# A kernel for attention and two expert layers: the first layer's opening and the order of its router's operations

## The chip, the core and the metric

The kernel runs on one core of a Trainium2 chip. The metric is the time of one execution on the device in microseconds, as the median of several runs.

The engines are named as in the profile: PE (TensorE, matrix products), DVE (VectorE), ACT (ScalarE), POOL (GpSimd, which also issues indirect transfers) and SP (SyncE, which issues plain transfers). Each works through its own list of instructions in the order in which it is written, and waits on semaphores for the others.

## What is computed

Attention over 4 batches, 12 heads, 448 positions and head width 64, then two layers of experts one after the other, each over the same 1792 tokens of width 768 with 8 experts of inner width 1024. All inputs and outputs are float32.

```python
scores = (q @ k.T) / sqrt(64), causal mask, softmax, @ v        # 4 x 12 heads
x = the heads side by side                                      # [1792, 768]

# first layer: the router compares directions
logits = (x / |x|) @ (emb / |emb|).T / tau
e = argmax(logits);  g = softmax(logits)[e]
x = g * (relu(x @ w1[e]) @ w2[e])

# second layer: the router is a product, with a bias by modality
logits = x @ w_gate + modality_bias[modality_id]
e = argmax(logits);  g = softmax(logits)[e]
out = g * (relu(x @ w1[e]) @ w2[e])
```

## The kernel before, in words

Everything that enters a large product is split into a high part (a rounded copy, `xh`, `w1h`, `w2h`, `hh`) and the rest (`xl`, `w1l`, `w2l`, `hl`). A product is then three: high by high, high input by low weight, low input by high weight. ACT makes the high parts by casting, DVE the low parts by subtracting.

**Attention** (loop at L799) goes through 24 pairs of heads in a software pipeline. Its last turns also bring the last batch of the first router: sums of squares (`route_ss`), transposes of x (`route_t`, L513) and the products for the logits (`route_l`, L524). `warm` (L783) puts products on PE whose result nobody reads.

**The router of the first layer** (`route1_head` L590, `route1_tail` L620, `finish_route` L193, `argmax` L208): transposed logits, scaling, argmax with a one-hot `r1ohb`, a count over tokens by products with `triu` and `ones` (L631, L633), slots, the softmax's value for the chosen expert (a subtraction, an exponential on ACT, a sum and a reciprocal), and a scatter of one row per token into a list by expert in DRAM (`meta1`). These functions are generators: each `yield` ends a step, and who drives them decides what stands between two steps. For the last batch the driver is `last_route1` (L1462).

**Tables.** `Lead.order` (L256) sorts the experts, `table` (L1220) turns counts into a list of blocks and issues the gathers of the next blocks' rows (`gather_m`, `gather_x`); its second half finds the second expert, whose number POOL copies (`load_second`, L1211) so that SP can load its weights. `switches` (L1265) writes `t_tab`, a table that says at each block whether the expert changes. The other engines read it into registers to branch.

**Blocks.** The first layer takes 128 tokens of one expert at a time. `first_block` (L1151) is block 0, `section(j)` (L1299) is block j. A block is two products with `w1` (`up`, L967, 18 matmuls each), a ReLU on ACT, transposes of the result (`h_transposes`, or `h_turn` and `h_turned`) and the product with `w2` (`down`, L1029, 48 matmuls). In section j the product with `w2` belongs to block j - 1. Where the expert changes, `split_next` (L1286) splits new weights, and `load_next` (L1198) issues the loads of the ones behind them. Block 0 begins while the router still finishes: `step()` in `first_block` runs one step of `last_route1` between two pieces of the block.

**The second router.** After a block of the first layer its outputs are routed for the second one: transposes (`route_t2`), logits (`route_l2`, product with `wg`), argmax to a one-hot `ob` (`route_a`, L1084), the count (`route_p`, L1105), slots and scatter (`route_b`). These are spread over the section of a later block. `prep(m, j)` (L948) makes `xh` and `xl` of block j; from block 3 on DVE first turns the gathered rows (`x_squares`, L945).

## Time and profile before

| | us |
|---|---|
| median of 3 runs | 942.31 |
| fastest, slowest run | 939.3, 949.46 |
| profiled execution | 932.79 |
| its span in the profile | 931.1 |
| PE, DVE, ACT, POOL busy in the span | 864.4, 699.8, 428.4, 478.0 |

The profile is one execution; times in it count from its span's start. Attention takes about the first 245 us, the first expert layer goes to about 620, the second one to the end. In a timeline a line gives the start, the time that it took, engine, source line, operation, output and inputs, how many in a row, and in brackets how long the engine stood before it and what released it. `issue` is time for which the profile shows no wait. Bracketed waits on an engine cost time only where another engine then waits for that one.

### The profile page before, as it was taken

What the parts mean: (1) busy time and instruction counts of PE and PEld (TensorE: products, weight loads), DVE (VectorE), ACT (ScalarE), POOL (GpSimd) and SP (SyncE); (2) the same over time, 40 slices, a digit from 0 to 9 for tenths busy, and PEclk for the clock granted to TensorE, in tenths of its full rate; (3) what the DMA queues carried; (4) which work ended last, traced back from release to release, by engine and by line L of the source; (5) the groups of instructions that cost most, each with busy time, mean ns of one, the idle gap of its engine ahead of it and who ended that gap; (6) DMA issues with size and microseconds to landing.
All of it is one profiled execution on the core that took longest, in us unless ns stands there. A gap on an engine that the chain in (4) does not pass through costs nothing. (4 is left out here: it accounts for less than half of the span.)

```text
span 931.1 us, 21180 instructions
## 1 busy us (share of the span) xinstructions
PE 864.4 (93%) x7010; PEld 752.0 (81%) x7010; DVE 699.8 (75%) x1800; ACT 428.4 (46%) x779; POOL 478.0 (51%) x477
## 2 busy tenths in 40 slices
PE   4999998988788999999999999979989999999994
PEld 3778777776576989988999888977779999898894
DVE  7999998997875766787657783467767578985793
ACT  3767866776434745575445552244111231412313
POOL 7867497674265153544645554312634454554541
PEclk9999998999899999999999999999989999999998
DMA  6899987889737765686515751110181115511110
GB/s 190 163 165 172 210 181 158 178 182 177 235 93 262 277 239 169 221 293 223 186 39 195 276 184 46 45 36 22 56 306 55 53 55 170 175 56 48 58 38 17
DMA packets 114454, 137.45 MB, mean 148 GB/s; under 512 B 78381, under 2 KB 82787, under 8 KB 114288
## 3 DMA queue, kind: packets, MB, share of 16 engines
q1 hardware_dynamic: 101376, 108.76, 42.8%
q0 software_dynamic: 12912, 26.83, 9.1%
q8 instruction: 61, 1.00, 0.4%
q14 instruction: 105, 0.86, 0.3%
HBM read 101.48 MB, written 19.92 MB: 130 GB/s over the span
## 5 line engine op out<-in xcount | busy, mean ns | idle before, releaser
L764 POOL DMA_INDIRECT xg<-x,xi x128 | 135.2, 1056 | 97.4 <-DMA x<-yb,mg 55.5
L973 PE MATMUL h<-w1h,xh 128*128 128x512 f32 x408 | 164.5, 403 | 1.9 <-ACT xh L957 1.1
L975 PE MATMUL h<-w1h,xl 128*128 128x512 f32 x408 | 161.1, 395 | 1.0 <-DVE xl L958 1.0
L974 PE MATMUL h<-w1l,xh 128*128 128x512 f32 x408 | 161.2, 395 | 0.7 <-DVE w1l L714 0.7
L1035 PE MATMUL o<-w2h,hh 128*128 128x384 f32 x528 | 140.4, 347 | 1.8 <-issue 1.6
L1035 PE MATMUL o<-w2h,hl 128*128 128x384 f32 x528 | 137.5, 341 | 2.7 <-DVE hl L988 1.5
L1035 PE MATMUL o<-w2l,hh 128*128 128x384 f32 x528 | 136.8, 340 | 1.4 <-issue 1.3
L1015 DVE STREAM_TRANSPOSE hs<-h 32x256 f32<-32x256 f32 x240 | 107.1, 446 | 21.5 <-PE h L975 8.3
L434 ACT ACTIVATE ex<-sc,nm 112x112 f32<-112x112 f32 (+1 forms) x192 | 83.9, 502 | 67.7 <-DVE nm L429 65.7
L1035 PEld LDWEIGHTS o<-w2h,hl 128*128 128x128 f32 x528 | 96.7, 190 | 3.6 <-DVE hl L988 2.1
L1035 PEld LDWEIGHTS o<-w2h,hh 128*128 128x128 f32 x528 | 95.8, 192 | 4.8 <-issue 3.0
L1035 PEld LDWEIGHTS o<-w2l,hh 128*128 128x128 f32 x528 | 97.1, 191 | 2.3 <-issue 1.8
L1021 ACT ACTIVATE hh<-hs 128x512 fp32r<-128x512 f32 x30 | 18.4, 630 | 174.1 <-PE o L1035 112.1
L975 PEld LDWEIGHTS h<-w1h,xl 128*128 128x128 f32 x408 | 76.9, 189 | 19.4 <-DVE xl L958 2.0
L974 PEld LDWEIGHTS h<-w1l,xh 128*128 128x128 f32 x408 | 77.2, 189 | 17.9 <-DVE w1l L714 2.6
L973 PEld LDWEIGHTS h<-w1h,xh 128*128 128x128 f32 x408 | 77.1, 189 | 17.7 <-ACT xh L957 1.3
L714 DVE TENSOR_TENSOR w1l<-w1r,w1h 128x1024 fp32r<-128x1024 f32 x66 | 76.6, 1220 | 9.3 <-ACT w1h L712 8.0
L429 DVE TENSOR_REDUCE nm<-sc 112x1 f32<-112x112 f32 (+1 forms) x192 | 75.1, 437 | 9.5 <-PE sc L424 8.7
L714 DVE TENSOR_TENSOR w2l<-w2r,w2h 128x768 fp32r<-128x768 f32 x82 | 72.4, 951 | 7.8 <-ACT w2h L712 6.8
L946 DVE STREAM_TRANSPOSE xr<-xg 128x768 f32<-128x768 f32 x32 | 52.0, 1626 | 22.6 <-DMA xg<-x,xi 15.8
L712 ACT CAST w1h<-w1r 128x1024 fp32r<-128x1024 f32 x64 | 62.5, 1047 | 9.5 <-PE h L975 5.0
L712 ACT CAST w2h<-w2r 128x768 fp32r<-128x768 f32 x82 | 61.5, 845 | 0.8 <-ACTq L1374 0.6
(327 smaller groups left out, 1919.2 us busy)
## 6 DMA issues: line engine op xcount, KB each, us to landing
w1r<-in_w1a SPq DMA_DIRECT2D x48, 512.0 KB
w2r<-in_w2a SPq DMA_DIRECT2D x64, 384.0 KB
r<-in_kqP SPq DMA_DIRECT2D x24, 448.0 KB
w1r<-in_w1b SPq DMA_DIRECT2D x18, 512.0 KB
w2r<-in_w2b SPq DMA_DIRECT2D x24, 384.0 KB
vr<-in_vh SPq DMA_DIRECT2D x24, 224.0 KB
x<-xb SPq DMA_DIRECT2D x16, 336.0 KB
xg<-x,xi POOLq DMA_INDIRECT x128
```

The costliest lines, as they stand in the source:

```text
L429: vec.tensor_reduce(out=nms[h][:, c : c + 1], in_=scs[h, c][:CP, : CP * (c + 1)], axis=AX.X, op=ALU.min)
L434: act.activation(dst, scs.pop((h, c))[:CP, :n], AF.Exp, bias=nms[h][:, c : c + 1], scale=-1.0)
L712: act.copy(hi[k], r[k])
L714: vec.tensor_sub(lo[k], r[k], hi[k].bitcast(F32))
L764: pool.indirect_dma_start(out=xgs[j % 3][:, q * (D // Q) : (q + 1) * (D // Q)], out_offset=None, in_=quarters, in_offset=IND(ap=xi[:, q : ...
L946: vec.transpose(xr.rearrange("p k (q r) -> p q k r", q=Q), xgs[j % 3].rearrange("p (q r k) -> p q k r", q=Q, k=KD))
L973: pe.matmul(hps, lhsT=xh[:, c], rhs=w1h[c][:, ns], start=(c == 0), stop=False)
L974: pe.matmul(hps, lhsT=xh[:, c], rhs=w1l[c][:, ns], start=False, stop=False)
L975: pe.matmul(hps, lhsT=xl[:, c], rhs=w1h[c][:, ns], start=False, stop=(c == KD - 1))
L1015: vec.transpose(hr[cols, :, rows], hps[rows, q * 256 : (q + 1) * 256].rearrange("p (c k) -> p k c", c=QR))
L1021: act.activation(hh[k], part, AF.Relu)
L1035: pe.matmul(ops[:, n, :384], lhsT=h[f // KH][:, f % KH], rhs=w[f][:, n * 384 : (n + 1) * 384], start=(f == 0 and st == 0), stop=(f == KF - ...
```

## The change

In the attention's last turns 15 more `warm` products are put on PE: 7 more ahead of the last transposes, 3 behind them and 5 behind the last logits. In block 0 the first product is `up_late`: all 12 matmuls of `xh` stand ahead of the 6 of `xl`. The router's last batch takes its logits and its argmax, up to the one-hot, in two steps ahead of the block's matmuls, without the expert order between its operations; the softmax's subtraction and exponential move ahead of the count; the expert order follows the scatter. Of `w2` in block 0 only slice 0 gets its low part early. `table` is cut in two by a `yield`: the half that finds the second expert, and with it POOL's copy, stands behind the low parts of `w2`. In section 1 the logits of the second router stand ahead of the transposes, and in section 2 `route_a` stands as a whole ahead of block 3's `prep`.

```diff
--- before.py
+++ after.py
@@ -624,6 +624,10 @@
         vec.tensor_copy(ohb[:, :NCH], oh[:CP])
         base = small.tile([P, E], F32, tag="r1base", name="r1base" + nm)
         vec.tensor_add(base, cnt1, slot8)
+        gate = finish_route(lg, mx, CP, NCH, nm, mts[b][:, :, 2])
+        if b == B - 1:
+            for _ in range(2):
+                next(gate)
         yield
         yield ALIGN
         pr = side()[:, : (NCH + 1) * E].rearrange("p (c e) -> p c e", e=E)
@@ -646,7 +650,7 @@
         vec.tensor_copy(si, sf)
         yield
         mt = mts[b]
-        yield from finish_route(lg, mx, CP, NCH, nm, mt[:, :, 2])
+        yield from gate
         if b == 0:
             yield from lead1.choose(cnt1)
         elif b == 1:
@@ -832,7 +836,7 @@
         if 0 <= t < NPR:
             halves_lo(t, (1,))
         if g == NPR + 2:
-            warm(ps_T, "T", WV)
+            warm(ps_T, "T", WV + 7)
         if 0 <= r < NPR:
             if r == NPR - 1:
                 for c in range(NCH):
@@ -840,6 +844,8 @@
                 last_root = route_root(B - 1)
                 next(last_root)
             route_t(r, xbs[r // PB])
+            if r == NPR - 1:
+                warm(ps_T, "T", 3)
             if r == NPR - 2:
                 for c in range(NCH):
                     route_ss(B - 1, c, xbs[B - 1], 1)
@@ -870,6 +876,8 @@
             values(v, 1)
         if 0 <= r < NPR:
             route_l(r)
+            if r == NPR - 1:
+                warm(ps_T, "T", 5)
         if 0 <= v < NPR:
             combine(v, xbs[v // PB])
         if g < NPR:
@@ -964,6 +972,19 @@
                 next(meanwhile, None)
             vec.tensor_sub(xl, xr, xh.bitcast(F32))
 
+    def up_late(j, n, between):
+
+        xh, xl = xhs[j % 2], xls[j % 2]
+        hps = ps_h.tile([P, 512], F32, tag="h", name="h")
+        ns = slice(n * 512, (n + 1) * 512)
+        for c in range(KD):
+            pe.matmul(hps, lhsT=xh[:, c], rhs=w1h[c][:, ns], start=(c == 0), stop=False)
+            pe.matmul(hps, lhsT=xh[:, c], rhs=w1l[c][:, ns], start=False, stop=False)
+        for c in range(KD):
+            between.get(c, lambda: None)()
+            pe.matmul(hps, lhsT=xl[:, c], rhs=w1h[c][:, ns], start=False, stop=(c == KD - 1))
+        return hps
+
     def up(j, n, between={}):
         xh, xl = xhs[j % 2], xls[j % 2]
         hps = ps_h.tile([P, 512], F32, tag="h", name="h")
@@ -1155,14 +1176,18 @@
         if not ahead:
             prep(m, 0)
             step()
-        split_away(range(0 if m.routed else 3, away))
-        h0 = up(0, 0, {2: step, 3: step} if ahead else {3: step})
+        if m.routed:
+            split_w(2, range(away), range(1))
+            h0 = up_late(0, 0, {2: step})
+        else:
+            split_away(range(3, away))
+            h0 = up(0, 0, {2: step, 3: step} if ahead else {3: step})
         split_w(2, range(away, KF if ahead else 6), ())
         if ahead:
             split_w(2, (), range(away, away + 2))
         step()
         relu(0, h0)
-        if not ahead:
+        if not ahead and not m.routed:
             split_w(2, (), range(away, away + 1))
         h1 = up(0, 1, {4: lambda: prep(m, 1), 5: step} if ahead else {4: step})
         relu(1, h1)
@@ -1171,8 +1196,10 @@
         h_transposes()
         if ahead:
             split_w(2, (), range(away + 3, KF))
+        if m.routed:
+            split_w(2, (6, 7), range(1, KF))
         drain(steps)
-        if not ahead:
+        if not ahead and not m.routed:
             split_w(2, (6, 7), range(away + 1, KF))
         if not ahead:
             switches(m, m.tab0)
@@ -1248,6 +1275,7 @@
                     gather(1)
             gather(2)
 
+        yield
         nz = small.tile([P, E], F32, tag="t_nz", name="t_nz" + m.m, bufs=1)
         vec.tensor_single_scalar(nz, m.nb, 0.5, op=ALU.is_ge)
         vec.tensor_tensor(out=t64, in0=m.lead.gt, in1=nz[:, None, :].to_broadcast([P, E, E]), op=ALU.mult)
@@ -1317,6 +1345,8 @@
                 m.gather_m(j + 4)
                 m.gather_r(j + 4)
             ra, rb = (route_a(), chain(route_g(), route_b())) if finish else (iter(()), iter(()))
+            if j == 2:
+                drain(ra)
             if FIRSTQ <= j + 1 < MAXB:
                 prep(m, j + 1, ra, FIRSTQ + 1)
             h0 = up(j, 0)
@@ -1355,10 +1385,11 @@
                 down(m, m.mg(j - 1), h_split)
             else:
                 if m.routed:
+                    route_l2()
                     h_turn()
                 (h_turned if m.routed else h_split)()
                 pass_on()
-            if begin:
+            if begin and j > 1:
                 route_l2()
             vec.tensor_copy(gt, m.mg(j))
 
@@ -1428,17 +1459,22 @@
         route_p()
         drain(route_b())
         yield
-        table(m2, both)
+        drain(table(m2, both))
 
     def last_route1(both):
         head = route1_head(B - 1)
-        for _ in range(2):
+        for _ in range(6):
             next(head)
         yield
-        together(head, lead1.order(cnt1))
+        drain(head)
         yield from (y for y in route1_tail(B - 1) if y == ALIGN)
         yield
-        table(m1, None)
+        drain(lead1.order(cnt1))
+        rest = table(m1, None)
+        next(rest)
+        yield
+        yield
+        drain(rest)
 
     drain(last_root)
     m1.gather_early((1,), 3 * S)
```

DVE in block 0, from the low part of x on (`ld_` is the expert order, `r1` and `am_` the router, `w2l` low weights), before:

```order
L958 TENSOR_TENSOR xl_5808<-xt,xh_5807 128x384 x2
L260 SCALAR_TENSOR_TENSOR ld_key<-cnt_194,iota_127 128x8
L605 COPY r1lor_5864<-t 112x32
L262 SCALAR_TENSOR_TENSOR ld_key<-ld_onem_212,ld_key 128x8
L607 TENSOR_TENSOR r1lgr_5845<-t,r1lor_5864 112x32
L264 TENSOR_TENSOR ld_mat<-ld_key 128x64
L613 TENSOR_TENSOR r1lgr_5845<-r1lgr_5845,r1nrr_5724 112x32
...
L624 CAST r1ohb_186<-am_ohr_5872 112x32
L626 TENSOR_TENSOR r1baser_5888<-cnt_194,slot_130 128x8
...
L723 TENSOR_TENSOR w2l_5799<-w2r_5496,w2h_5801 128x768
L723 TENSOR_TENSOR w2l_5800<-w2r_5497,w2h_5802 128x768
L636 TENSOR_TENSOR r1slr_5910<-t,r1baser_5888 112x32
```

DVE at the same place now:

```order
L605 COPY r1lor_5868<-t 112x32
L607 TENSOR_TENSOR r1lgr_5862<-t,r1lor_5868 112x32
L613 TENSOR_TENSOR r1lgr_5862<-r1lgr_5862,r1nrr_5731 112x32
L966 TENSOR_TENSOR xl_5825<-xt,xh_5824 128x384 x2
L215 TENSOR_REDUCE am_mxr_5884<-r1lgr_5862 112x4
...
L624 CAST r1ohb_186<-am_ohr_5885 112x32
L626 TENSOR_TENSOR r1baser_5893<-cnt_194,slot_130 128x8
L196 TENSOR_TENSOR fr_shr_5895<-r1lgr_5862,am_mxr_5884 112x32
L718 TENSOR_TENSOR w2l_5816<-w2r_5496,w2h_5818 128x768
L640 TENSOR_TENSOR r1slr_5922<-t,r1baser_5893 112x32
...
L206 RECIPROCAL mt_160<-fr_smr_5930 112x4
L260 SCALAR_TENSOR_TENSOR ld_key<-cnt_194,iota_127 128x8
```

Three router operations come ahead of `xl`, the others behind it in one piece, the subtraction for the exponential (`fr_shr`) ahead of the first `w2l`, and the order (`ld_key`) behind the reciprocal that ends the softmax.

DVE further on in block 0, now: behind the last operation of the table's first half stand `hl`, seven `w2l` (three of them shown) and the table's second half up to `ld_mxm`, from which the second expert's number is copied. Before, the second half stood ahead of `hl`.

```order
L1267 TENSOR_SCALAR t_idqm_322<-t_basem_5975,qrow 128x22
...
L1009 TENSOR_TENSOR hl_5811<-ht,hh_5813 128x512
L1009 TENSOR_TENSOR hl_5812<-ht,hh_5814 128x512
L718 TENSOR_TENSOR w2l_5817<-w2r_5497,w2h_5819 128x768
L718 TENSOR_TENSOR w2l_5786<-w2r_5498,w2h_5820 128x768
...
L718 TENSOR_TENSOR w2l_5781<-w2r_5503,w2h_5787 128x768
...
L1280 TENSOR_SCALAR t_nzm_6042<-t_nbm_319 128x8
L1281 TENSOR_TENSOR t_64m_5965<-ld_gtm_216,t_nzm_6042 128x64
L1282 TENSOR_REDUCE t_nxem_323<-t_64m_5965 128x8
...
L1288 TENSOR_REDUCE ld_mxm_214<-t_nzm_6042 128x1
```

All that finds the second expert has moved behind the low weights.

ACT in block 0, before (`fr_shr` is the exponential, `xh` and `w2h` are casts):

```order
L957 CAST xh_5807<-xt 128x384 x2
L722 CAST w2h_5801<-w2r_5496 128x768
L722 CAST w2h_5802<-w2r_5497 128x768
L198 ACTIVATE fr_shr_5918<-fr_shr_5918 112x32
L712 CAST w2h_5803<-w2r_5498 128x768
```

and ACT in block 0 now:

```order
L965 CAST xh_5824<-xt 128x384 x2
L198 ACTIVATE fr_shr_5895<-fr_shr_5895 112x32
L716 CAST w2h_5818<-w2r_5496 128x768
L716 CAST w2h_5819<-w2r_5497 128x768
L716 CAST w2h_5820<-w2r_5498 128x768
```

The exponential has moved ahead of the first two casts of `w2h`.

DVE in section 2 (`xr` and `xl` are block 3's x, the others but `gt` belong to `route_a`), before:

```order
L1363 COPY gt<-mg_340 128x8
L946 STREAM_TRANSPOSE xr<-xg_338 128x4x6x32
L1088 TENSOR_SCALAR r2md<-yq 128x1
L1090 TENSOR_SCALAR r2bs<-mb,r2md 128x8
L1092 SCALAR_TENSOR_TENSOR r2bs<-mb,yq,r2bs 128x8
L965 TENSOR_TENSOR xl_5763<-xr,xh_5762 128x768
L1096 TENSOR_TENSOR lg_5786<-pl,r2bs 128x8
L215 TENSOR_REDUCE mx_5788<-lg_5786 128x1
```

and DVE in section 2 now:

```order
L1394 COPY gt<-mg_340 128x8
L1109 TENSOR_SCALAR r2md<-yq 128x1
L1111 TENSOR_SCALAR r2bs<-mb,r2md 128x8
L1113 SCALAR_TENSOR_TENSOR r2bs<-mb,yq,r2bs 128x8
L1117 TENSOR_TENSOR lg_5803<-pl,r2bs 128x8
...
L1122 CAST ob_5801<-oh_5799 128x8
L1123 COPY yo_5797<-yq 128x8
L954 STREAM_TRANSPOSE xr<-xg_338 128x4x6x32
L973 TENSOR_TENSOR xl_5780<-xr,xh_5779 128x768
```

`route_a` with its one-hot `ob` now ends ahead of `xr`.

## Rows read from the trace of the kernel before

**Rows 1.** Windows view: stretch, busy us of PE (x instructions), PEclk, DMA share, GB/s

```profile
250.00:255.00 5.00, 3.97 (x11) 0.50 0.35 129
```

**Rows 2.** Timeline of PE, end of attention and block 0

```profile
242.23 1.47 PE L787 MATMUL warm<-mask,ones 112*128 112x512 bf16 x6
245.11 0.60 PE L517 MATMUL tb<-ident,xb 112*128 112x112 f32 x4 [1.41 <-DVE xb L508]
...
248.61 0.36 PE L601 MATMUL t<-ident,lgs 16*112 16x16 f32 x4 [1.24 <-issue]
...
252.69 0.80 PE L975 MATMUL h<-w1h,xl 128*128 128x512 f32 x1 [1.01 <-DVE xl L958]
...
255.88 0.19 PE L631 MATMUL t<-r1ohb,triu 112*128 112x40 bf16 x1
...
262.17 0.40 PE L975 MATMUL h<-w1h,xl 128*128 128x512 f32 x1
...
266.50 0.61 PE L1035 MATMUL o<-w2h,hl 128*128 128x384 f32 x2 [0.90 <-DVE hl L988]
```

**Rows 3.** Timeline of DVE, block 0

```profile
252.08 1.02 DVE L958 TENSOR_TENSOR xl<-xt,xh 128x384 fp32r<-128x384 f32 x2 [0.57 <-ACT w2h L722]
253.02 0.16 DVE L260 SCALAR_TENSOR_TENSOR ld_key<-cnt,iota 128x8 f32<-128x8 f32 x1
...
255.50 0.23 DVE L282 TENSOR_TENSOR ld_gtm<-ld_gtm,ld_key 128x64 f32<-128x64 f32 x1
...
258.77 0.18 DVE L202 TENSOR_REDUCE fr_smr<-fr_shr 112x4 f32<-112x32 f32 x1 [0.30 <-ACT fr_shr L198]
258.99 0.17 DVE L204 TENSOR_SCALAR fr_smr<-fr_smr 112x4 f32<-112x4 f32 x1
...
264.68 0.16 DVE L1260 TENSOR_REDUCE ld_mxm<-t_nzm 128x1 f32<-128x8 f32 x1
...
265.77 1.28 DVE L988 TENSOR_TENSOR hl<-ht,hh 128x512 fp32r<-128x512 f32 x2
266.96 4.42 DVE L714 TENSOR_TENSOR w2l<-w2r,w2h 128x768 fp32r<-128x768 f32 x5
...
274.37 0.14 DVE L1284 CAST t_tabm<-t_chgm 1x1 int32<-1x1 f32 x1
```

**Rows 4.** Timeline of ACT, casts of block 0 and x of block 1

```profile
250.88 1.57 ACT L722 CAST w2h<-w2r 128x768 fp32r<-128x768 f32 x2
...
275.82 0.86 ACT L957 CAST xh<-xt 128x384 fp32r<-128x384 f32 x2 [0.27 <-issue]
```

**Rows 5.** Timeline of PE, blocks 1 to 4

```profile
276.35 0.50 PE L973 MATMUL h<-w1h,xh 128*128 128x512 f32 x1 [1.11 <-ACT xh L957]
...
302.04 0.17 PE L1108 MATMUL pr<-ob,triu 128*128 128x8 bf16 x1 [1.42 <-DVE ob L1101]
...
308.03 0.52 PE L1035 MATMUL o<-w2h,hl 128*128 128x384 f32 x2
308.38 1.06 PE L997 MATMUL ht<-ident,hs 128*128 128x128 f32 x8
...
317.64 1.12 PE L1071 MATMUL yt<-ident,yb 128*128 128x128 f32 x6
```

**Rows 6.** Timeline of POOL, the second expert's number

```profile
272.23 0.18 POOL L164 TENSOR_SCALAR t_secondm<-ld_mxm 1x1 int32<-1x1 f32 x1
```

**Rows 7.** Timeline of SP, loads of weights

```profile
274.54 6.24 SPq L701 DMA_DIRECT2D w1r<-in_w1a  x6
291.53 5.73 SPq L701 DMA_DIRECT2D w2r<-in_w2a  x8
```

**Rows 8.** Timelines of ACT and DVE, the third expert's weights

```profile
311.95 2.15 ACT L712 CAST w1h<-w1r 128x1024 fp32r<-128x1024 f32 x2 [1.04 <-SPq L1294]
...
316.86 1.23 DVE L1005 TENSOR_TENSOR hl<-ht,hh 128x512 fp32r<-128x512 f32 x2
```

## The prediction

> **What bounds the kernel now.** I read four views: busy time by stretch, then the timelines of TensorE (PE), VectorE (DVE) and the queues from the end of attention to the fourth block of the first expert layer. Past that the change moves nothing.
>
> In [rows 1] the granted clock is 0.50 from 250 to 255 us: the lower level, 1.2 GHz. Ahead of it PE had stood still for 1.41 us and for 1.24 us [rows 2]. In the same stretch PE waits 1.01 us for `xl`, at 255.88 for the one-hot of the router, and at 266.50 another 0.90 us for `hl`; 27 matmuls of block 0's first product still lie between 255.88 and 262.17 [rows 2].
>
> The reader should see in [rows 3] who makes PE wait: DVE. It starts on the block's work at 252.08 and has hardly a gap until 274.51, when the table that the other engines branch on (`t_tab`) is written. Block 1 hangs on that table too: ACT reads it ahead of its `xh`, and PE starts block 1 at 276.35 [rows 4, 5].
>
> In the third block PE waits 1.42 us for the routing one-hot `ob` at 302.04; the 12 pairs of matmuls that follow until 308.38 take 6.3 us, where pairs at full clock start 0.35 us apart, 4.2 us in all [rows 5]. The wait and the lower clock cost 3.5 us together.
>
> Beside that runs a second chain. POOL copies the number of the second expert at 272.23 [rows 6]; SP issues that expert's first weights at 274.54, its second weights at 291.53, and the third expert's first weights behind them [rows 7]. They land so late that ACT still waits at 311.95; DVE gets to `hl` at 316.86, and PE's transposes at 317.64, which need a bank that `hl` frees, start when the first half of `hl` is done [rows 5, 8]. PE's own work ended there too, so the two chains meet with no slack: after 317 the later one counts.
>
> **The change, part by part.** All of it is weighed against the profiled execution, 932.79 us with a span of 931.1; the runs' median, 942.31, is 1.0102 times that.
>
> *Fillers.* One costs about 0.22 us (1.47 for six). Thirteen in place of six end at 242.23 + 13 x 0.218 = 245.06, just under the 245.11 at which PE gets its `xb` [rows 2]: free. Three fill the wait for ACT behind these transposes: free to about 0.1. Five, 1.1 us, stand ahead of PE's branch into the expert layer, behind which L601 started at 248.61 with 1.24 us of waiting for its queue [rows 2]. They cost between nothing and 1.1 us; I take 1.1, since the branch is read in order. It does no harm: the first reader of L601's result is DVE at 252.08. If the clock stays up, the high products start near 250.5 as before.
>
> *High part first.* The 12 products of `xh` need no `xl`: the 1.01 us goes. At full clock (0.235 each) they end near 253.4. What is late next is the one-hot. DVE now does three steps of the logits ahead of `xl` and five of the argmax behind it, at 0.22 each (258.77 to 258.99 [rows 3]), and 0.94 for `xl` (252.08 to 253.02): 252.08 + 0.66 + 0.94 + 1.10 = 254.8, written by 255.0. PE's count starts 0.9 us earlier than 255.88 and 22 matmuls remain in place of 27, another 1.2: about 2 us gained on PE at the end of block 0's first product.
>
> *The shorter router chain.* Here DVE pays. Before, the router's eight steps ran between the twelve of the expert order: 20 operations from 253.02 to 255.73, 0.135 each [rows 3]. Now they stand in two chains in which each waits for the one ahead: eight at 0.22 are 1.7 us that the interleaving had hidden. Second, the exponential now stands ahead of ACT's first two casts of `w2h`, which in the kernel before were done at 250.88 [rows 4]. ACT stands until the router's subtraction, about 255.2, then does the exponential (0.2) and a cast (0.85), while DVE's next instruction is `w2l` of that cast: DVE idles about 1.1 us, with the slots, the scatter and the table queued behind it. Against that goes the 0.30 us wait at 258.77, now covered. Ledger: +1.7 + 1.1 - 0.3 = +2.5; added up step by step I get +2.8; I take +2.6 for the end of DVE's list, and 0 to +3 as its bounds (nothing lost; both losses in full).
>
> A rule speaks for the lower bound. The Trainium skill, VectorE: DVE Perf Modes, section The DRAIN you can't avoid, says that the next operation starts only when the pipeline is empty, whether or not it depends on the last. By it, interleaving hid nothing, and the 1.7 would be 0 (rival B). The 0.135 against 0.22 in the rows above disagrees, so I go by the rows.
>
> *Where the loss lands.* `hl` comes ahead of the second half of the table: from the ledger about 264.7 in place of 265.77, so PE still keeps 1.1 us at 266.50. But the eight operations that find the second expert, done at 264.84 before, now stand behind `hl` (1.2) and seven `w2l` (0.885 each, five in 4.42 [rows 3], 6.2 in all): they end near 273.9, and `t_tab` near 277.1. So:
> - POOL's copy, 272.23 before, comes at about 274.0: its scatters and gathers start earlier, but it now waits for DVE. The weight chain is 1.8 us late. Bounds: -1.1 (no DVE loss) to +2.2.
> - ACT's `xh` of block 1 came 1.3 us behind `t_tab` (274.51 to 275.82 [rows 3, 4]), part of it the end of `yb`. Now 277.1 + 0.6 to 1.3: 277.7 to 278.4. PE starts block 1 about 2 us later than 276.35, and what block 0 gained is gone. Before that it stands some 3.5 us, and the clock may fall again: for as long as it ran low at 302 that costs some 2 us.
>
> *Third block.* `ob` now stands ahead of the transpose of x (about 1.6 us) and the subtraction (0.95) on DVE, so it is ready before PE finishes its product: the 1.42 goes, and with it the low clock, 3.5 us in all. Behind `ob` now wait block 3's `xr` and `xl`, and on ACT the two ReLUs behind `xh`, some 2.5 us later; their next readers are PE's transposes at 308.38 and the next block: covered. The router's logits ahead of the transposes in block 1 only fill a gap, since the product behind them waits for `w1l` on DVE: 0.
>
> **The sum.** PE alone: +2.0 at block 1, between 0 and +2 for the clock there, -3.5 at the third block: -1.5 to +0.5 at 317. The weight chain: +1.8. The later one counts, so PE waits again at 317.64, for weights. 932.79 + 1.8 = 934.6; times 1.0102: **944.1 us**, 0.2% slower. About 1%, 9.4 us, is what a measurement of this kernel can tell from no change.
>
> **Rivals.**
> A, the forecast: 944.1.
> B, DVE loses nothing by the split chains (the rule above): only 1.1 - 0.3 remain, the copy comes at about 272.2 as before: 932.8, so 942.3. For it: the rule, and that a step of the order alone may follow faster than 0.22. Against: the spacing in [rows 3].
> C, the weight chain does not meet PE: with the gathers of blocks 1 and 2 earlier, the transfer has the queues to itself and makes up its late start. Then PE's -1.5 counts: 931.3, so 940.8. For it: 17 us lie between SP's two rows [rows 7]. Against: the wait at 311.95.
> D, slower: the wait ahead of block 1 drops the clock and keeps it down as long as in the opening, near 6.5 us, so half of it, 3.3, is lost; PE is 5.3 late, and from there on it is PE that decides, since 5.3 - 3.5 = 1.8 equals the weights' delay. If the clock falls at 302 all the same, only 1.4 comes back: +3.9, 936.7, so 946.3.
> E, the fillers don't hold the clock: the 12 high products take 0.43 each, the count starts near 257, 2.1 later than forecast, and table and copy with it: 932.79 + 1.8 + 2.1 = 936.7, so 946.3.
>
> **Chances.** A 0.46, B 0.18, C 0.16, D 0.12, E 0.08. The range takes in all five with some 3 us on either side for the spread of runs (939.3 to 949.46): 937.5 to 949.0. None of the cases reaches 9.4 us; what is left beyond 1% is that spread, and for faster C and B together with the whole 3.5 and 2.0: 0.06 faster, 0.05 slower, 0.89 the same.
>
> **What would show it.** Right: full clock from 249 to 256; `xl` no longer waited for; a gap on DVE ahead of the first `w2l`, released by ACT; POOL's copy waiting for DVE near 274; PE idle for over 3 us ahead of block 1; no wait for `ob`; a new wait at the fourth block's transposes. Wrong: `t_tab` written before 275, or the second expert's weights issued no later than 274.5 on this axis. Then the gains in the opening and the third block reach the end, and the kernel is faster than I say.

## The result, and the profile after

| | kernel before | changed kernel |
|---|---|---|
| median of 21 runs, us | 936.89 | 943.42 |
| lowest, highest | 932.37, 949.46 | 938.12, 950.73 |
| profiled execution, its span | 932.79, 931.1 | 941.0, 939.3 |

The changed kernel takes 1.0077 times as long, with a 95% interval of 1.0054 to 1.0099: some 7 us more. The three runs shown ahead of the prediction had a median of 942.31, so the time of before stood 5 us too high there.

In the profile of after the first of the fillers in the attention's last turn starts at 243.80, in that of before at 242.23 [rows 2]. These 1.6 us lie ahead of every edit and are no part of the change. So all times are compared from that filler on. This is the timeline of PE in the changed kernel, with the columns of [rows 2]:

```profile
243.80 2.98 PE L791 MATMUL warm<-mask,ones 112*128 112x512 bf16 x13
248.78 1.25 PE L791 MATMUL warm<-mask,ones 112*128 112x512 bf16 x5
256.49 0.19 PE L635 MATMUL t<-r1ohb,triu 112*128 112x40 bf16 x1 [0.94 <-DVE r1ohb L624]
266.81 0.61 PE L1056 MATMUL o<-w2h,hl 128*128 128x384 f32 x2 [1.77 <-DVE hl L1009]
278.56 1.04 PE L963 MATMUL xt<-ident,xg 128*128 128x128 f32 x6 [1.49 <-issue]
294.45 0.50 PE L994 MATMUL h<-w1h,xh 128*128 128x512 f32 x1 [1.72 <-issue]
308.21 0.62 PE L1056 MATMUL o<-w2h,hh 128*128 128x384 f32 x2 [1.85 <-ACTq L1318]
323.60 1.12 PE L1092 MATMUL yt<-ident,yb 128*128 128x128 f32 x6
526.21 1.11 PE L1092 MATMUL yt<-ident,yb 128*128 128x128 f32 x6 [1.41 <-DVE hl L1026]
```

The wait for `xl` is gone, and so is the wait for `ob` at the third block. PE now waits for the one-hot (0.94), longer for `hl` (1.77 in place of 0.90), ahead of block 1 (1.49), ahead of section 2 (1.72), and ahead of that section's product with `w2` (1.85). Behind the wait for `hl` the granted clock falls to 0.50, the lower level of 1.2 GHz, where in the kernel before it stays at 1.00 (PE by stretch: busy time, granted clock, DMA share, GB/s):

```profile
269.31:271.81 2.50, 2.50 (x10) 0.50 0.00 0
```

The last row of the timeline, far behind the place of the change, is a wait that the kernel before does not have there.

On DVE, timeline with the columns of [rows 3]:

```profile
255.14 0.17 DVE L215 TENSOR_REDUCE am_mxr<-r1lgr 112x4 f32<-112x32 f32 x1
255.35 0.19 DVE L217 TENSOR_TENSOR am_ohr<-r1lgr,am_mxr 112x32 f32<-112x32 f32 x1
...
257.62 0.96 DVE L718 TENSOR_TENSOR w2l<-w2r,w2h 128x768 fp32r<-128x768 f32 x1 [1.02 <-ACT w2h L716]
...
258.60 0.15 DVE L642 TENSOR_TENSOR cnt<-cnt,t 128x8 f32<-128x8 f32 x1
...
259.76 0.13 DVE L260 SCALAR_TENSOR_TENSOR ld_key<-cnt,iota 128x8 f32<-128x8 f32 x1
...
266.07 1.28 DVE L1009 TENSOR_TENSOR hl<-ht,hh 128x512 fp32r<-128x512 f32 x2
...
274.93 0.16 DVE L1288 TENSOR_REDUCE ld_mxm<-t_nzm 128x1 f32<-128x8 f32 x1
...
278.08 0.14 DVE L1312 CAST t_tabm<-t_chgm 1x1 int32<-1x1 f32 x1
```

The argmax's steps follow each other 0.21 us apart, and DVE stands 1.02 us ahead of the first `w2l`, as forecast. The fourth and fifth rows hold what the prediction had overlooked: the expert order begins with `ld_key<-cnt`, and it now stands behind `cnt<-cnt,t`, the operation that adds the last batch. In the kernel before the order stood ahead of the count ([rows 3] at 253.02). It sorted the experts by the counts of three batches, and now sorts them by those of four.

POOL, after:

```profile
268.15 6.13 POOL L749 DMA_INDIRECT mg<-meta,t_idxm  x1 [0.30 <-DMA meta<-mt,r1sir]
274.59 0.95 POOL L752 DMA_INDIRECT xg<-x,mg  x1 [0.30 <-issue]
...
276.85 0.18 POOL L164 TENSOR_SCALAR t_secondm<-ld_mxm 1x1 int32<-1x1 f32 x1
```

One gather took 6.13 us, where the others of this place, in all runs but one, take 0.9 to 1.7, and the copy of the second expert's number ([rows 6]) waits behind it. So does the gather of block 1's x (274.59), and PE's transposes of it at 278.56 come behind 1.49 us of standing.

### What the new order does

The reference's routing of the given inputs shows why the order differs. The last batch sends 419 of its 448 tokens to expert 5, which until then has 45. By three batches' counts the kernel before takes the experts 2, 0, 1, 7, 3, 5, 6, 4, with 2, 1, 3, 1, 1, 4, 1, 5 blocks. By four batches' counts the changed one takes 2, 0, 5, 7, 1, 6, 3, 4, with 2, 1, 4, 1, 3, 1, 1, 5. Two experts of one block stand next to each other at blocks 6 and 7 before, at 11 and 12 now. In the section of the second of the two, DVE makes low parts of `w2` for one expert and of `w1` for the next. Section 12 is also `LATE`, where DVE sorts the experts of the second layer. DVE in section 7 of before:

```profile
400.15 7.04 DVE L714 TENSOR_TENSOR w2l<-w2r,w2h 128x768 fp32r<-128x768 f32 x8 [1.40 <-ACT w2h L712]
...
409.67 6.90 DVE L714 TENSOR_TENSOR w1l<-w1r,w1h 128x1024 fp32r<-128x1024 f32 x6 [0.34 <-issue]
...
417.96 1.25 DVE L1005 TENSOR_TENSOR hl<-ht,hh 128x512 fp32r<-128x512 f32 x2
```

and in section 12 of after (`ld_key` and `ld_gtm` are the second layer's order):

```profile
505.78 7.04 DVE L718 TENSOR_TENSOR w2l<-w2r,w2h 128x768 fp32r<-128x768 f32 x8 [2.39 <-ACT w2h L716]
...
512.81 0.16 DVE L260 SCALAR_TENSOR_TENSOR ld_key<-cnt,iota 128x8 f32<-128x8 f32 x1
...
515.52 0.22 DVE L282 TENSOR_TENSOR ld_gtm<-ld_gtm,ld_key 128x64 f32<-128x64 f32 x1
...
517.11 6.90 DVE L718 TENSOR_TENSOR w1l<-w1r,w1h 128x1024 fp32r<-128x1024 f32 x6 [0.39 <-issue]
...
525.40 1.26 DVE L1026 TENSOR_TENSOR hl<-ht,hh 128x512 fp32r<-128x512 f32 x2
```

In the former `w1l` starts 9.5 us behind the start of `w2l`, in the latter 11.3, with the order between them, and `hl` follows 17.8 and 19.6 us behind it. Both end in a wait of 1.41 us for `hl` on PE, the later one in a longer section. Two tables by stretch, each from one set of transposes (`yt`) to the next, price it. Before, the sixth to the seventh set, then the eleventh to the twelfth and on to the thirteenth:

```profile
397.45:418.76 21.31, 19.91 (x113) 17.76 (x112) 18.82 (x36) 16.31 (x24) 11.44 (x9) 1.00 0.83 284
...
497.88:517.60 19.72, 19.72 (x113) 17.91 (x112) 14.73 (x47) 10.70 (x16) 9.49 (x8) 1.00 0.52 174
517.60:537.62 20.02, 20.00 (x114) 17.83 (x113) 13.94 (x36) 10.79 (x18) 12.58 (x13) 1.00 0.65 230
```

After, the same three:

```profile
403.66:423.38 19.72, 19.72 (x114) 17.95 (x112) 14.44 (x38) 10.71 (x16) 10.55 (x9) 1.00 0.61 199
...
502.19:526.21 24.02, 21.73 (x114) 17.36 (x112) 20.79 (x52) 16.45 (x24) 13.29 (x11) 1.00 0.73 237
526.21:547.60 21.39, 20.32 (x112) 17.96 (x113) 15.55 (x44) 11.35 (x19) 9.86 (x10) 1.00 0.74 258
```

The columns behind the length are the busy times of PE, its weight loads, DVE, ACT and POOL, the granted clock, and the DMA's share and rate. The first stretch is 1.6 us shorter, the other two are 4.3 and 1.4 longer, at full clock: 4.1 us lost together.

### The profile page after: what moved, and what is told of

It is laid out like the page before. It is cut to its first block, busy times and chain, and to the rows that moved or that the text cites. A ratio compares the mean times of both kernels' runs of the same rounds, so it can differ in the third digit from the quotient of the medians.

```text
span 939.3 us, 21207 instructions
## 1 busy us (share of the span) xinstructions
PE 873.0 (93%) x7025; PEld 756.9 (81%) x7025; DVE 700.8 (75%) x1800; ACT 428.7 (46%) x779; POOL 481.5 (51%) x477
## 5 line engine op out<-in xcount | busy, mean ns | idle before, releaser
L994 PE MATMUL h<-w1h,xh 128*128 128x512 f32 x402 | 161.9, 403 | 2.7 <-issue 1.9
L995 PE MATMUL h<-w1l,xh 128*128 128x512 f32 x402 | 159.1, 396 | 1.8 <-DVE w1l L718 1.0
L996 PE MATMUL h<-w1h,xl 128*128 128x512 f32 x402 | 158.6, 395 | 0.0
```

Of the source, the lines that this page charges most:

```text
L994: pe.matmul(hps, lhsT=xh[:, c], rhs=w1h[c][:, ns], start=(c == 0), stop=False)
L995: pe.matmul(hps, lhsT=xh[:, c], rhs=w1l[c][:, ns], start=False, stop=False)
L996: pe.matmul(hps, lhsT=xl[:, c], rhs=w1h[c][:, ns], start=False, stop=(c == KD - 1))
```

## The experiments

Each run's ratio is to runs of the kernel before on the same chip. That kernel's median was 924.6 us on the chip of the first four kernels (second early to copy first), 925.0 on that of the next four (to after again), and 936.7 and 937.7 on a third chip, that of the last four. How far a ratio carries from one chip to another is seen at the mended kernel, which ran on two. The marks come from one profile each: us from the first filler to the count (`triu`), to the end of DVE's table (start of its last write to `t_tab`), to POOL's copy, to block 1's first product, to the first and second set of transposes, and the length of two later stretches.

| kernel | ratio, 95% interval | count | t_tab | copy | block 1 | yt 1 | yt 2 | yt 6-7 | yt 11-12 |
|---|---|---|---|---|---|---|---|---|---|
| before | 1 | 13.65 | 32.14 | 30.00 | 34.12 | 38.49 | 75.41 | 21.3 | 19.7 |
| after | 1.0077, 1.0054 to 1.0099 | 12.69 | 34.28 | 33.05 | 35.97 | 40.33 | 79.80 | 19.7 | 24.0 |
| second early | 1.0055, 1.0020 to 1.0091 | 12.69 | 34.22 | 28.63 | 36.45 | 40.82 | 77.71 | 19.7 | 24.5 |
| third alone | 1.0002, 0.9966 to 1.0037 | 13.64 | 32.13 | 29.98 | 34.08 | 38.42 | 73.78 | 21.3 | 19.7 |
| second late | 0.9986, 0.9953 to 1.0020 | 13.64 | 32.12 | 29.98 | 34.06 | 38.41 | 77.79 | 21.3 | 19.7 |
| copy first | 1.0010, 0.9976 to 1.0044 | 13.64 | 32.10 | 22.70 | 35.87 | 40.27 | 75.60 | 21.3 | 19.7 |
| after, old order | 1.0024, 0.9996 to 1.0053 | 12.69 | 34.19 | 31.33 | 34.48 | 41.12 | 78.20 | 21.3 | 19.7 |
| before, new order | 1.0036, 1.0002 to 1.0071 | 13.65 | 32.15 | 30.01 | 34.11 | 38.46 | 76.43 | 19.7 | 24.4 |
| mended | 0.9978, 0.9947 to 1.0009 | 12.69 | 32.28 | 29.73 | 32.56 | 37.59 | 73.73 | 21.7 | 19.7 |
| after again | one run, 926.83 us | 12.69 | 34.20 | 31.34 | 34.73 | 39.53 | 74.93 | 19.7 | 24.4 |
| casts first | 1.0028, 0.9991 to 1.0066 | 12.68 | 33.38 | 30.52 | 33.19 | 40.03 | 76.74 | 21.3 | 19.7 |
| no fillers | 1.0032, 1.0002 to 1.0063 | 12.70 | 32.29 | 29.73 | 32.64 | 39.21 | 76.14 | 21.7 | 20.0 |
| combined | 1.0049, 1.0019 to 1.0078 | 12.70 | 31.02 | 30.32 | 36.11 | 42.51 | 79.42 | 21.7 | 20.8 |
| mended again | 1.0032, 1.0002 to 1.0063 | 12.70 | 32.29 | 29.74 | 32.68 | 38.99 | 75.31 | 21.7 | 20.3 |

**Second early.** The table in one piece again:

```diff
-        rest = table(m1, None)
-        next(rest)
-        yield
-        yield
-        drain(rest)
+        drain(table(m1, None))
```

> The changed kernel, but with the table's two halves in one piece, so that the eight operations that find the second expert stand ahead of the low parts of hl and w2 as in the kernel before. W (the weights' chain sets the time: POOL's copy of the second expert's number, SP's loads, ACT's casts): the copy is no longer held by DVE and comes near 272 to 274 us, hl some 2 us later than in the changed kernel, and the ratio to the kernel before falls from 1.008 to 0.998 to 1.003. P (PE's own stalls ahead of block 1 and the clock there set it): nothing of that goes, the ratio stays at 1.006 to 1.010.

The copy came 1.4 us earlier than in the kernel before, and the ratio is 1.0055: outside W's range, and just below P's, with an interval that reaches into both. In exchange PE waits 3.38 us for `hl`. Nothing here shows that the late copy is the loss. The two columns on the right were not yet part of any theory.

**Third alone.** The kernel before with the edits in sections 1 and 2:

```diff
+            if j == 2:
+                drain(ra)
...
                 if m.routed:
+                    route_l2()
                     h_turn()
...
-            if begin:
+            if begin and j > 1:
```

> The kernel before with the changed order in sections 1 and 2 alone (route_l2 ahead of h_turn, route_a ahead of the third block's x). W: the 1.42 us wait for ob and the low clock behind it go, but the transposes of block 2's output still start near 317.6, since the weights come no earlier; ratio 0.998 to 1.001. P: the 3.5 us reach the end; ratio 0.995 to 0.997.

The wait for `ob` is gone, the time is the same. In place of it PE waits 1.78 us in that section for ACT. PE, then DVE and ACT ahead of it:

```profile
305.79 0.62 PE L1035 MATMUL o<-w2h,hh 128*128 128x384 f32 x2 [1.78 <-ACTq L1290]
```

```profile
302.47 0.24 DVE L1101 CAST ob<-oh 128x8 bf16<-128x8 f32 x1
...
302.68 1.59 DVE L946 STREAM_TRANSPOSE xr<-xg 128x768 f32<-128x768 f32 x1
```

```profile
304.37 0.83 ACT L962 CAST xh<-xr 128x768 fp32r<-128x768 f32 x1 [6.63 <-DVE xr L946]
305.11 0.59 ACT L979 ACTIVATE hs<-h 128x512 f32<-128x512 f32 x1
```

With `route_a` ahead, `xr` stands behind `ob` on DVE, ACT's `xh` behind `xr`, and the first ReLU (`hs`) behind `xh`. PE's product with `w2` starts 0.09 us behind the end of that ReLU. It does so, by 0.09 to 0.10 us, in all ten kernels that have this edit, with a wait of 1.78 to 1.98 us; in the four that don't, the ReLU had ended over 2.1 us before the product. The profile here names ACT's sequencer, at the branch on new weights, as what PE waited for; that the branch is late because of the ReLU ahead of it is read from these times.

**Second late.** The kernel before with the table cut, meant to put its second half behind the low parts of `w2`:

```diff
+        yield
         nz = small.tile([P, E], F32, tag="t_nz", name="t_nz" + m.m, bufs=1)
...
+        if m.routed:
+            split_w(2, (6, 7), range(away + 1, KF))
         drain(steps)
-        if not ahead:
+        if not ahead and not m.routed:
...
-        table(m1, None)
+        rest = table(m1, None)
+        next(rest)
+        yield
+        drain(rest)
```

> The kernel before with one thing moved: the eight operations that find the second expert stand behind hl and the low parts of w2. W: the copy moves from 272.2 to 274 or later, the loads with it, and the transposes at 317.6 by 2 to 4 us; ratio 1.002 to 1.005. P: hl comes 2 us earlier and the 0.90 us wait at 266.5 goes, the rest is hidden; ratio 0.997 to 1.000.

The edit did less than that. In the trace DVE's second half still stands ahead of `hl` and of five low parts of `w2`; a single `w2l` has moved ahead of it:

```profile
264.09 0.16 DVE L1263 TENSOR_REDUCE ld_mxm<-t_nzm 128x1 f32<-128x8 f32 x1
264.56 1.29 DVE L988 TENSOR_TENSOR hl<-ht,hh 128x512 fp32r<-128x512 f32 x2 [0.32 <-ACT hh L987]
265.77 4.42 DVE L714 TENSOR_TENSOR w2l<-w2r,w2h 128x768 fp32r<-128x768 f32 x5
```

The second expert's number is found 23.0 us behind the filler, where it is 22.5 in the kernel before and 31.1 in the changed one. The copy stays at 29.98, behind POOL's two pairs of gathers. So neither theory was put to the test: what a late second half costs, this run does not say.

**Copy first.** POOL's copy and SP's loads ahead of the gathers:

```diff
-        for gather in (m.gather_m, m.gather_x):
-            if not both:
-                with late():
-                    gather(1)
-            gather(2)
...
         if not both:
             load_second(m)
+        for gather in (m.gather_m, m.gather_x):
+            if not both:
+                with late():
+                    gather(1)
+            gather(2)
```

> The kernel before with the copy of the second expert's number, and the loads that hang on it, ahead of the gathers of blocks 1 and 2 on POOL (DVE's order is the same). W: the copy comes near 266 in place of 272.2 and the first loads some 6 us earlier; block 1's gather is 0.5 us later or meets the weights on the DMA queues; the weights are in time at 317.6, and PE's own chain counts: ratio 0.995 to 1.000. P: no gain, block 1's x is later: 1.000 to 1.004.

The copy came 7.3 us earlier; block 1 started 1.75 later, for its gather; the second transposes came 35.3 us behind the first in place of 36.9; no gain in time. It neither shows nor excludes that the weights hold the third block, since what they may have given was spent ahead of block 1.

**After, old order,** and **before, new order.** One line each, and not one instruction:

```diff
-PLACES = (0, 7, 2, 4, 6, 5, 3, 1)
+PLACES = (0, 7, 5, 2, 4, 6, 3, 1)
```

```diff
-PLACES = (0, 7, 2, 4, 6, 5, 3, 1)
+PLACES = (0, 7, 4, 6, 5, 2, 3, 1)
```

> The changed kernel with other numbers in PLACES, so that the expert order computed from the counts of all four batches comes out as the order that the kernel before gets from three batches; no instruction differs. O (the change lets the expert order read the updated counts; another sequence of experts and blocks, with the two one-block experts that follow each other at blocks 11 and 12 in place of 6 and 7, costs time late in the layer): the wait of 1.41 us for hl returns to the seventh block's transposes, the stretch from the seventh to the twelfth falls from 102.8 us to 98.8, the sixth to the seventh rises from 19.7 to 21.3; ratio falls from 1.008 to 1.004 to 1.006. P (the opening alone is the loss): stretch lengths and ratio stay, 1.006 to 1.010.

> The kernel before with other numbers in PLACES, so that its order from three batches' counts comes out as the changed kernel's order; no instruction differs. O: opening and DVE as before, the stretch from the seventh to the twelfth block's transposes rises from 98.8 to 102.8 us, the sixth to the seventh falls from 21.3 to 19.7; ratio 1.002 to 1.004. P: 0.999 to 1.001.

Both came out as O says, stretch by stretch, as the table shows; the first ratio, 1.0024, lies below O's range and P's, the second, 1.0036, in O's. From the sixth set of transposes to the thirteenth it is 143.6 to 144.0 us in the four profiles with the new sequence, and 139.8 to 142.8 in the ten with the old one, whatever the opening. What follows the fourteenth set is no longer with the new sequence, on the chip that ran both: 363.7 and 365.0 us to the end of the span, against 365.0 and 365.4. So the price lies in the first layer. The kernel before with the new order has the waits of after in its sets of transposes:

```profile
424.29 0.82 PE L1071 MATMUL yt<-ident,yb 128*128 128x128 f32 x6
...
527.52 1.11 PE L1071 MATMUL yt<-ident,yb 128*128 128x128 f32 x6 [1.42 <-DVE hl L1005]
```

The seventh set does not wait, the twelfth does. Its ratio is 1.0036, clear of 1 by its interval: that is what the sequence of experts alone costs.

**Mended.** DVE's and ACT's losses taken back; the expert order reads three batches' counts again:

```diff
             prep(m, 0)
+            if m.routed:
+                split_w(2, range(away), ())
             step()
         if m.routed:
-            split_w(2, range(away), range(1))
+            split_w(2, (), range(1))
...
-        yield from (y for y in route1_tail(B - 1) if y == ALIGN)
+        tail = route1_tail(B - 1)
+        while next(tail) != ALIGN:
+            pass
         yield
-        drain(lead1.order(cnt1))
+        together(lead1.order(cnt1), tail)
+        yield
```

> The changed kernel with the first two casts of w2h ahead of the exponential on ACT, and the twelve operations of the expert order interleaved with the slots and the softmax's sum, so that the order reads the counts of three batches again. If the forecast's ledger for DVE holds, the wait ahead of the first w2l (1.02 us) and 0.8 us of the chain go: t_tab ends 32.2 to 32.5 us behind the fillers in place of 34.3, block 1 starts at 34.2 to 34.6 in place of 36.0 to 36.4. With O the late stretch is as in the kernel before too: ratio 0.998 to 1.002. If the loss lies elsewhere (fillers, high part first), 1.004 to 1.008.

The table ended at 32.28, as expected, and block 1 started at 32.56, earlier than expected and 1.56 us ahead of the kernel before. The ratio is at the lower end of the first range, with an interval that holds 1.

**After again.**

> The changed kernel once more, unchanged. If the 6.13 us of POOL's second gather belong to the kernel, they return, with the copy 33 us behind the fillers; if they are chance, the gather takes about 1.0 to 1.4 us and the copy comes at 30.5 to 32, held by the gathers or by DVE.

The long gather did not return. The time, 926.83 us, is 1.0020 of the median of the kernel before on that chip, and within the runs of the old order there (923.0 to 930.6). POOL waits for DVE, and the copy comes 31.34 us behind the filler:

```profile
273.11 0.20 POOL L164 TENSOR_SCALAR t_secondm<-ld_mxm 1x1 int32<-1x1 f32 x1 [1.76 <-DVE ld_mxm L1288]
```

**Casts first.** The first of the mended kernel's two hunks on top of the old order.

> The changed kernel with the old expert order (by PLACES, as in the run before) and one edit of the mended one: the first two casts of w2h stand ahead of the exponential on ACT. By the ledger, which splits the loss on DVE into a wait for ACT (1.0 us) and the dependent steps of the two chains (1.7 us less what the order's own steps gain), the wait of 1.02 us ahead of the first w2l goes and nothing else: t_tab ends 33.1 to 33.4 us behind the fillers, between 34.2 and the mended kernel's 32.3; ratio 0.999 to 1.002. If the wait was the whole of it, t_tab ends at 32.3 and the ratio is the mended kernel's, 0.997 to 0.999.

The table ended at 33.38: 0.8 us from the wait for ACT, and the other 1.1 (to 32.28) from interleaving alone. That is seen on DVE here and in the last run, mended again. In each fence the first row begins the 20 operations of the slots, the softmax's sum and the expert order, and the second row follows them:

```profile
255.80 0.18 DVE L640 TENSOR_TENSOR r1slr<-t,r1baser 112x32 f32<-112x32 f32 x1
...
259.79 0.27 DVE L1253 TENSOR_TENSOR t_km<-cnt,jp 128x112 f32<-128x112 f32 x1
```

```profile
256.56 0.16 DVE L260 SCALAR_TENSOR_TENSOR ld_key<-cnt,iota 128x8 f32<-128x8 f32 x1
...
259.30 0.27 DVE L1253 TENSOR_TENSOR t_km<-cnt,jp 128x112 f32<-128x112 f32 x1
```

They take 4.0 us chain behind chain and 2.7 interleaved. The ratio, 1.0028, is above what either theory gave; its interval takes in most of the first range and nothing of the second.

**No fillers.** The mended kernel with `WV + 7` back to `WV` and without the two other calls of `warm`.

> The mended kernel without the 15 added fillers. If they hold the clock: the granted clock falls to 0.50 between about 248 and 255 us, the 12 products of the high part take 0.43 us each in place of 0.23, which the 0.94 us wait for the one-hot hides in part; the count starts 1 to 2 us later behind the attention's end, t_tab by 0 to 1 us; ratio 0.998 to 1.001. If the fillers only cost their own time (1.1 us ahead of the branch), the ratio falls to 0.996 to 0.998.

Without the fillers the clock falls, as in the kernel before. PE by stretch, from 5 us behind the first filler on (busy, granted clock, DMA):

```profile
249.90:254.90 5.00, 3.54 (x15) 0.68 0.91 359
```

and of the last run, the mended kernel with them:

```profile
247.68:252.68 5.00, 4.38 (x24) 1.00 0.86 337
```

Yet count, table, copy and start of block 1 are the same to 0.04 us; the count was expected 1 to 2 us later. What PE loses at the lower clock it would have spent waiting for the one-hot. The ratio came out at 1.0032, above both ranges.

**Combined.** The mended kernel with the two halves of the table interleaved, all ahead of `hl`, and the copy between the kinds of gathers:

```diff
+        together(first(), second())
...
         for gather in (m.gather_m, m.gather_x):
...
+            if gather == m.gather_m and not both:
+                load_second(m)
```

> The mended kernel with the table's two halves interleaved step by step on DVE, all ahead of hl, and POOL's copy between the two kinds of gathers. By the ledger t_tab ends 31.5 to 32.0 us behind the fillers (32.3 in the mended one), the copy near 26 (29.7), the first weights of the second expert some 3 us earlier, block 1 starts no later, and the 1.86 us wait for the second expert's second weights gets shorter: ratio 0.993 to 0.997. If the weights' chain is not what holds the third block, 0.996 to 0.999.

The table ended earlier still, 31.02, and all was lost again to a gather that took 5.48 us:

```profile
267.30 5.48 POOL L749 DMA_INDIRECT mg<-meta,t_idxm  x1 [1.86 <-DVE w2l L718]
```

Block 1's x came late, PE stood 4.71 us ahead of it, and the copy came no earlier. Whether the timed runs all had that gather is not known.

**Mended again.**

> The mended kernel once more, since the runs of the call before (casts first, no fillers, combined) were all slower than the kernel before. If the mended kernel's ratio of 0.998 is its own, it returns, 0.996 to 1.000, and the fillers and the shorter table are what differs; if the level of a call shifts all ratios of kernels with the changed opening, it comes out at 1.002 to 1.005. In the trace the ledger says the same of both: t_tab 32.3 us behind the fillers, block 1 at 32.6 to 34.6.

The second expectation held: on a chip where the kernel before takes 937 us, the mended kernel is at 1.0032, like the one without fillers. No version is shown to beat the kernel before.

## Why the prediction was right, and where it was not

The forecast was 0.2% slower, from 1.8 us; the measured time lies in its range, and the change moved the way it says. But 0.77% is four times that size, and part of the agreement in microseconds comes from the high median that it started from. The mechanism behind the 1.8 us, weights that come late to the third block, is not shown, and what costs most was not in the sum: that the time lies in the range is in part luck.

- **"Past that the change moves nothing."** This step failed. Reading the order of instructions showed that the twelve operations of the expert order had moved behind the count; that they read the count, and so another value, was not asked. A run without any changed instruction shows the price: 1.0036 for the new sequence in the kernel before. The old one in the changed kernel gives 1.0024; but the 1.0077 beside it was measured where the kernel before took 936.9 us, not 925.0, and the changed kernel's one run on the chip of the old order (1.0020) doesn't tell the two apart. In the profiles of before and after it is 4.1 us, with its end some 220 us behind the last row that the prediction looked at.
- **The ledger for DVE.** Forecast +2.6 us for the end of the table, measured +2.1 (34.28 against 32.14). Its terms stand in kind: the wait for ACT is 1.02 us (forecast 1.1), and taking it away gives 0.8 back; the split chains, forecast 1.7, give 1.1 back when they are interleaved. Rival B, that the split chains cost nothing, falls with this: the same operations, only ordered otherwise, end 1.1 us earlier (33.38 to 32.28). The Trainium skill, VectorE: DVE Perf Modes, section The DRAIN you can't avoid, says that the next operation does not start until the pipeline is empty; by that alone the two orders would have ended together, and the trace disagrees. The section adds that an operation that is not held starts earlier, which the prediction left out; so the page does not stand against the rows.
- **PE's gain in block 0.** The count starts 1.0 us earlier (12.69 against 13.65), forecast 0.9, and the transposes behind the products with `w1` 2.1 (18.88 against 21.02), forecast 2. At `hl`, 1.26 us are left (23.01 against 24.27), forecast 1.1. What the prediction had not seen is the fall of the clock behind that wait: the product with `w2` starts its last pair at 32.76, in the kernel before at 31.71. So PE's gain was gone ahead of block 1, and the 3.5 us of standing there, forecast as a sign, are 1.49.
- **"PE starts block 1 about 2 us later."** Measured 1.85, but not by the forecast's cause. In that profile PE waits for block 1's x behind the long gather, not for an `xh` behind the table: its transposes start 3.0 us behind the end of that x's gather, as they do in no fillers, combined and mended again. Where no gather is long, block 1 starts 0.6 us later (after again) and 0.4 (old order). So the 1.85 is luck.
- **The copy.** Forecast 1.8 us later. Without the long gather it is 1.3 (31.34 against 30.00), with it 3.05. The profile with it also has the wait of 1.72 us ahead of section 2, which no other has, and its second transposes are 4.4 us late where the first were 1.8; in after again they are 0.5 early.
- **"The weight chain meets PE, so the later one counts."** Not shown. The copy 1.4 us early (second early) recovered nothing clear of the intervals, and 7.3 us early (copy first) gained nothing that can be measured, with a loss of its own beside it. The new wait forecast for the fourth block's transposes is not in the profile of after; in casts first and mended again PE waits 1.12 and 0.74 us for `hl` there. Left open.
- **The third block.** That its 3.5 us would not reach the end is borne out: with that edit alone, 1.0002 (0.9966 to 1.0037). But a step of the forecast failed here: what now stands behind `ob`, the two ReLUs on ACT among it, was called covered until PE's transposes. PE's product with `w2` waits for ACT until the first of them is done, 1.85 us in the profile of after where the wait for `ob` had been 1.42. Only the low clock is gone: in third alone the pairs behind start 0.35 us apart.
- **The fillers.** The transposes that follow the thirteen start 2.88 us behind the first one in either kernel, so these are free, as forecast. They hold the clock, so rival E falls; and they are worth nothing here, which the prediction did not say.
- **Rival D** had a chance of 0.12 and is half there. Block 1's first product to the first transposes takes 4.37 us in the kernel before. It takes 6.3 to 6.8 in five kernels with the changed opening (old order, casts first, no fillers, combined, mended again), and the clock is low there. PE has stood 1.1 to 4.7 us ahead of block 1 in these five; the wait alone doesn't decide it, since the profile of after has 1.49 us and then 4.36 at full clock. The last run, from 30 us behind the filler on:

```profile
272.68:277.68 5.00, 3.02 (x11) 0.84 0.79 244
277.68:282.68 5.00, 4.80 (x21) 0.82 1.00 345
```

In the kernel before both are at full clock:

```profile
272.23:277.23 5.00, 3.89 (x22) 1.00 0.72 239
277.23:282.23 5.00, 4.76 (x25) 1.00 0.88 273
```

The mended kernel, run again, starts block 1 1.4 us ahead of the kernel before, and comes to the first transposes 0.5 us behind it. In the first profile of the mended kernel the same stretch took 5.03 us at full clock. So of what DVE's mending gave, some 1.3 us went with the clock, and 0.7 were lost at full clock too. This is the nearest reason for 0.9978 on the one chip and 1.0032 on the other, but it is argued from two profiles, not shown.

Of the 0.77%, 0.36 are the sequence, measured in the kernel before. The opening with the old sequence is 0.24 (interval -0.04 to 0.53), and so not shown to cost anything. Both were measured where the kernel before took 925.0 us, the 0.77 where it took 936.9. The rest is within the intervals, and the long gather may be part of it; its cause stays open.

## What to carry to other kernels

When instructions move, ask of each what it reads, and who writes that between its old place and its new one: a legal move past a write changes a decision that the kernel takes at run time, and its price can lie hundreds of microseconds later. A table of constants that undoes the decision, with every instruction left in place, measures it cleanly. Ask also who reads what is pushed behind the moved instructions: here a wait of 1.42 us taken away came back as one of 1.85. Look in the trace whether an edit moved what it was meant to move before reading its time. And where one engine is full from end to end of a stage, as DVE in block 0 here, holding the clock of another gave nothing.

## What the runs showed of the hardware that was not expected

**A gather that ends just behind a run of subtractions.** In the profile of after, POOL's gather starts at 268.15 beside a run of `w2l` on DVE, and ends at 274.28. The run ends at 273.43. In the combined kernel a gather of 5.48 us ends at 272.78, beside a run whose end is 271.67. The run of after, then that of the combined kernel:

```profile
267.27 6.16 DVE L718 TENSOR_TENSOR w2l<-w2r,w2h 128x768 fp32r<-128x768 f32 x7
```

```profile
265.51 6.16 DVE L718 TENSOR_TENSOR w2l<-w2r,w2h 128x768 fp32r<-128x768 f32 x7
```

In both the gather ended about 1 us after the run (0.85 and 1.11), which is near what one takes with no such run beside it (0.9 to 1.0). In the other profiles gathers beside the same run took 1.0 to 1.7 us. The Trainium skill, SBUF — State Buffer, section Who interferes with whom, says that a VectorE instruction with two inputs in SBUF, as `w2l` has, contends with a GpSimd instruction that reads SBUF, and not with one that only writes it. No row here shows whether the gather is such a reader. That a gather is held through several instructions, and only in 2 of 14 profiles, the section does not say, and no run here tells why.
